# First two operands of the third product's batch 0 made one quarter earlier in the second product

## Chip, cores and metric

The kernel runs on one core of one Trainium2 chip. The metric is device time in microseconds (us): the median of several executions. Times in the profile are those of one profiled execution.

## What is computed

Attention with a hash mask over 2 batches, 8 heads, 768 tokens and 64 dims, then two feed-forward layers on the 1536 x 512 result. This case lies in the feed-forward part:

```python
def _moe_ref(x, w1, w2, w3, w_out):
    h = np.maximum(np.maximum(x @ w1, x @ w2), x @ w3)
    return (h @ w_out).astype(np.float32)

def _moe2_ref(x, w_in, w_out):
    h = x @ w_in
    relu6 = np.clip(h + 3.0, 0.0, 6.0)
    g = h * relu6 / 6.0
    return (g @ w_out).astype(np.float32)

x = np.ascontiguousarray(attn_out.transpose(0, 2, 1, 3)).reshape(B * S, H * D)
x = _moe_ref(x=x, **moe_kwargs)
return _moe2_ref(x=x, **moe2_kwargs)
```

## The kernel before

Every fp32 matrix is kept as two parts in a matmul type, a high part (a copy by ScalarE into that type) and a low part (the matrix less its high part, by VectorE or GpSimd). A product of two matrices is three matmuls: high by high, high by low, low by high. The first product is `x` by `w1`, `w2`, `w3`; the second is `h` by the first layer's `w_out`; the third is the second's result by `w_in`; the fourth is the gated result by the last `w_out`.

**The second product** runs in four quarters, one for each batch `b` and half `dh` of the 512 columns, in the order `(b, dh)` = (0,0), (0,1), (1,1), (1,0). A quarter has two column tiles `d` of 128. A column tile is six steps `f` of six matmuls each (L1453, tiles `c`, `m`, `x` in PSUM), and then ScalarE copies it out into the resident tensor `xF` (L1481; in the last quarter L1473 to L1478). Four generators are advanced between the steps:

- `making` (the count a step is in `MK`, 3 in the quarters in question) makes the operands of the third product;
- `tick2` (the count is in `TQ`, by quarter, column tile and step) advances the jobs that bring weights on: `words` decodes one tile of raw words (ScalarE L954 and L956, VectorE L961 and L965) that SyncE has loaded into one of two buffers `wraw` (L918); `pjob` makes a set of seven weight operands for the third product (GpSimd L1006 and L1019, ScalarE L1015, and VectorE L1019 for the one low part that `WL` gives it); `ojob` and `wjob` make high and low parts of a plain tile (ScalarE L982 and L1070, GpSimd L984 and L1073);
- `sets0`, in the last quarter alone, runs the third product's first two sets, so that its matmuls (L1210) stand between those of the last quarter.

**The third product** multiplies blocks of 256 by 256 with seven products instead of eight (`seven`). Its right-hand operands of a batch are seven tiles of 128x768: B11, T1, T2, B21, T3, B22 and T4, of which the T's are differences of blocks. `xops` makes them one after the other, in the order that it is given:

```python
if sub:
    dve.tensor_tensor(out=B[i], in0=B[sub[0]], in1=B[sub[1]], op=ALU.subtract)    # L1161
    yield
act.activation(out=hi, in_=B[i], func=AF.Copy)                                     # L1164
yield
(dve if XE[n] else pool).tensor_tensor(out=lo, in0=B[i], in1=f32(hi), op=ALU.subtract)  # L1166
```

For batch 0 this begins at the end of the second quarter: B11 and T1 are made of the columns of the first quarter, which are in `xF` since the second quarter's beginning, and the other five also need those of the second. The differences overwrite blocks of `xF` (T1 is B12 - B11 in B11's place), and T4 is made from T2's difference. In the trace and the orders below the pairs (high, low) are B11 `xh2`/`xl2`, T1 `xh3`/`xl3`, T2 `G0`/`G1`, B21 `G2`/`G3`, T3 `T3`/`T8`, B22 `T2`/`T7`, T4 `G4`/`G5`. The third product's first set of weights is in `wh3`, `wl3`, `woh1` and others, its second in `G8` to `G11`.

`seven` starts with the product A11 by B11 in a tile `m`, ScalarE copies it to a tile `c` (L1216), and the next product is added onto that copy; a product into another tile `x` lies between, which ScalarE copies out too (L1221). VectorE then adds (L1224, L1230).

All engines take their instructions in program order. Nothing sorts them: the order of the generators' steps is the order on each engine.

Of the kernel before, what the change touches and what calls it, by code (L numbers as in the profile page):

```python
# [61 lines left out]
XS = 0  # L62
WL = (1, 0, 0, 0, 0)
WH = 2
TQ = (((2, 1, 2, 1, 2, 1), (2, 1, 2, 1, 2, 1)), ((1, 1, 1, 1, 1, 2), (1, 1, 1, 1, 1, 1)), ((1, 1, 1, 1, 1, 1), (1, 1, 1, 1, 1, 1)), ((1, 1, 1, 1, 0, 1), (1, 0, 2, 1, 1, 1)))
TS = 0
IS = 2
PR = (3, 4)
# [22 lines left out]
NW = 8  # L91
PJ = 4
LAGO = 1
XO = ((0, 1, 2, 3, 4, 5, 6),)
TN = (0, 1, 1)
OG = (1, 1, 1, 1)
PSB = (("s", 2, 2), ("x", 1, 1), ("m", 3, 1))
# [2 lines left out]
def f32(ap):  # L100
    return ap if ap.dtype == F32 else ap.bitcast(F32)
# [3 lines left out]
def body(ctx, tc, qT, kT, vP, projT, wts, consts, out):  # L105
# [26 lines left out]
    def units(tags=None):  # L132
        if not tags:
            tags = ring["order"][ring["n"] % len(ring["order"])]
            ring["n"] += 1
        if len(tags) == 2:
            return [unit(t) for t in tags]
        t = unit(tags)
        return [t[:, 0, :], t[:, 1, :]]
# [12 lines left out]
    def hsl(hf):  # L152
        return slice(hf * HF, (hf + 1) * HF)
# [101 lines left out]
    def blk(b, n):  # L255
        return X[:, 4 * b + 2 * (n // 2):4 * b + 2 * (n // 2) + 2, hsl(n % 2)]
# [665 lines left out]
    def moe(es, yp, wo, wx):  # L922
# [227 lines left out]
        def xops(b, tl, order):  # L1150


            B = [blk(b, n) for n in range(4)] + [blk(1 - b, n) for n in range(2)]
            S = (
                ("B11", 0, None), ("T1", 0, (1, 0)), ("T2", 4, (3, 0)), ("B21", 2, None),
                ("T3", 1, (3, 1)), ("B22", 3, None), ("T4", 5, (2, 4)),
            )
            for n in order:
                k, i, sub = S[n]
# [3 lines that stand above are left out]
                hi, lo = (x.rearrange("p (a b) -> p a b", a=2) for x in tl[n])  # L1163
# [3 lines that stand above are left out]
                x2[b][k] = tuple([x[:, i, :] for i in range(2)] for x in (hi, lo))  # L1167
                yield
# [129 lines left out]
        def xlate(places):  # L1298

            for k, n in (("T3", 1), ("T4", 2)):  # L1300
                B = blk(1, n)
                t = [[x[:, 0:HF] for x in places.pop(0)] for _ in range(2)]
                for j in range(2):
                    act.activation(out=t[j][0], in_=B[:, j, :], func=AF.Copy)
                    yield
                yield
                for j in range(2):
                    if j:
                        yield
                    dve.tensor_tensor(out=t[j][1], in0=B[:, j, :], in1=f32(t[j][0]), op=ALU.subtract)  # L1310
                xa[1][k] = tuple([t[j][i] for j in range(2)] for i in range(2))
                yield

        xt = [list(zip(xh0, xl0)), [(T[4], T[9]), (T[0], T[5]), (G[0], G[1]), (G[2], G[3])]]
        free = G[4:]
# [36 lines left out]
        def xmake():  # L1352
            for _ in range(4):
                yield
            thi(0, "T4")
            yield
            for k in ("T1", "T3"):
                xsum(1, k)
                yield
                yield  # L1360
            tlo(0, "T4", dve)
            yield
            for k in ("T2", "T4"):
                xsum(1, k)
                yield
            for k in ("T1", "T2"):
                thi(1, k)
                yield
                yield
                tlo(1, k, dve)  # L1370
                yield

        making = xmake()
# [27 lines left out]
        while lanes:  # L1401
            for i, g in enumerate(list(lanes)):
                if step < 24 - LN and i:
                    continue
                while next(lanes[i], 0) == 0:
                    if i == 0 and not late:
                        for _ in making:
                            pass
                        making, late = itertools.chain(hsplits.pop(0), xlate([*Wsl[3:6], wo[2]])), True
# [25 lines left out]
        def wout(i, last):  # L1435
            if last and i not in done_w:
                done_w.add(i)
                slots.append(weight2(("w", i)))
            return weight2(("w", i))

        making = iter(())
        g0, g1 = [], []
        sets0 = itertools.chain(inset(0, 0, g0, "m", "x"), inset(1, 0, g1, "m", "x"))
        for b, dh in ((0, 0), (0, 1), (1, 1), (1, 0)):
            for d in (2 * dh, 2 * dh + 1):
                us = units(("cc", "mm")[d] if (b, dh) == (1, 0) else None)
                for f in range(6):
                    wh, wl = wout(18 + 3 * dh + f // 2, b == 1 and d % 2 and f % 2)
                    c = slice(256 * (f % 2) + 128 * (d % 2), 256 * (f % 2) + 128 * (d % 2) + 128)
                    a, l = hT[f, b]  # L1450
                    for i, (w, r) in enumerate(((wh, a), (wh, l), (wl, a))):
                        for u, rh in zip(us, r):
                            pe.matmul(  # L1453
                                u[:, 0:HF], w[:, c], rh, start=f + i == 0, stop=f == 5 and i == 2
                            )
                    for _ in range(MK[3 * b + dh - 2 * b * dh]):
                        next(making, None)
                    tick2(TQ[3 * b + dh - 2 * b * dh][d % 2][f])
                    if (b, dh) == (1, 0) and 6 * d + f >= IS:
                        for _ in range(IN[6 * d + f - IS]):  # L1460
                            next(sets0, None)
                if (b, dh) == (1, 0):

                    if d == 0:
                        for _ in making:
                            pass
                        hi, lo = (
                            x.rearrange("p (a b) -> p a b", a=2) for x in (free.pop(0), free.pop(0))
                        )
                        x2[1]["B11"] = tuple([x[:, j, :] for j in range(2)] for x in (hi, lo))  # L1470
                    u0, u1 = (u[:, 0:HF] for u in us)
                    b11, t1, t3, b22 = (blk(1, n)[:, d, :] for n in (0, 0, 1, 3))
                    act.activation(out=hi[:, d, :], in_=u0, func=AF.Copy)  # L1473
                    act.activation(out=b11, in_=u0, func=AF.Copy)
                    dve.tensor_tensor(out=lo[:, d, :], in0=u0, in1=f32(hi[:, d, :]), op=ALU.subtract)
                    dve.tensor_tensor(out=b11, in0=u1, in1=b11, op=ALU.subtract)
                    dve.tensor_tensor(out=t3, in0=b22, in1=u1, op=ALU.subtract)
                    dve.tensor_tensor(out=blk(0, 0)[:, d, :], in0=u0, in1=t3, op=ALU.add)  # L1478
                    continue
                for hf in range(2):  # L1480
                    act.activation(out=X[:, 4 * b + d, hsl(hf)], in_=us[hf][:, 0:HF], func=AF.Copy)  # L1481
            if (b, dh) == (0, 0):
                while ("w", 23) not in held2:
                    tick2()
                h2 = slots.pop(0)
                s4 = wo[1]
                pslots.append({
                    "A": wo[0], "B": slots.pop(0), "S2": tuple(x[:, 0:256] for x in h2),
                    "S1": tuple(x[:, 0:256] for x in s4), "S4": tuple(x[:, 256:512] for x in s4),
                })  # L1490
            if (b, dh) == (0, 1):
                for _ in making:
                    pass
                making = xops(0, [(free.pop(0), free.pop(0)) for _ in range(7)], XO[0])
                free += own[0]
                a, b_ = ((free.pop(0), free.pop(0)) for _ in range(2))
                pslots.append({
                    "A": tuple(x[:, 0:512] for x in a), "B": tuple(x[:, 0:512] for x in b_),
                    "S1": tuple(x[:, 512:768] for x in a), "S4": tuple(x[:, 512:768] for x in b_),
                    "S2": tuple(x[:, 256:512] for x in h2),  # L1500
                })
            if (b, dh) == (1, 1):
                oslots += [slots.pop(0), slots.pop(0)]
                for _ in making:
                    pass
                tl = {n: (free.pop(0), free.pop(0)) for n in (3, 5)}
                making = xops(1, tl, (3, 5))
                g0 += [(free.pop(2), free.pop(2)) for _ in range(2)]
# [6 lines left out]
        making = xrest(1, tl)  # L1515
# [157 lines left out]
```

## Time and profile before

| | us |
|---|---|
| median of 3 executions | 688.95 (688.47 to 689.98) |
| the profiled execution | 690.18 |
| its span (first to last instruction) | 688.40 |
| TensorE matmuls busy | 666.0 (97%) |
| VectorE busy | 511.0 (74%) |
| ScalarE busy | 432.8 (63%) |
| GpSimd busy | 334.3 (49%) |
| mean granted clock of TensorE | 0.993 |

The profile has a page of sums, and the trace behind it can be asked for the waits (who waited for whom, in all), the chain of waits (the work that ended last, followed back), a timeline of single instructions, and the busy time of each engine in chosen stretches with TensorE's granted clock. In a timeline a bracket behind a row gives the idle time of the engine ahead of that row and what ended it. TensorE's matmuls overlap: they take 0.33 us each and start 0.17 us apart.

### The profile page before, as it was taken

Reading aid. Unit: us, or ns where it says so; the run is one execution under the profiler, and the core shown is the slowest. Engines: PE = TensorE matmul, PEld = TensorE weight load, DVE = VectorE, ACT = ScalarE, POOL = GpSimd, SP = SyncE. Lnnn points to the kernel's source line nnn. Section 1 sums busy time; section 2 is a strip of 40 time slices with the busy share of each in tenths; the row PEclk is TensorE's granted clock in tenths of the full one; section 3 lists DMA queues with packets and bytes.
Section 4 is the critical chain, followed back from the end, with each engine's and each line's share of the span. In section 5 each row is a group of like instructions: output and inputs, shape, how many; then the busy total and the mean of one; then the engine's idle time right before and its main releaser. Section 6 shows DMA issues by size and latency. Waiting matters only on the chain.

```text
span 688.4 us, 13482 instructions
## 1 busy us (share of the span) xinstructions
PE 666.0 (97%) x5189; PEld 613.2 (89%) x5189; DVE 511.0 (74%) x978; ACT 432.8 (63%) x749; POOL 334.3 (49%) x280
## 2 busy tenths in 40 slices
PE   8999999999999999999999996999999999999997
PEld 7789898888898989999999996989989889889986
DVE  6888988989985647677668477773868687877664
ACT  6667788889887525574746556676556565655520
POOL 6778898999987330654443543112142331313100
PEclk9999999999999999999999998999999999999999
DMA  6665557767441000211223222010203020211004
GB/s 191 170 153 136 160 123 184 191 167 190 103 90 63 2 1 32 92 62 62 62 92 120 96 64 89 31 62 1 92 30 123 31 92 31 92 61 62 1 0 184
DMA packets 22527, 61.80 MB, mean 90 GB/s; under 512 B 3864, under 2 KB 4952, under 8 KB 22464
## 3 DMA queue, kind: packets, MB, share of 16 engines
q1 hardware_dynamic: 22032, 60.55, 30.7%
q8 instruction: 41, 0.67, 0.4%
q10 hardware_dynamic: 432, 0.40, 0.2%
q14 instruction: 22, 0.18, 0.1%
HBM read 38.87 MB, written 3.15 MB: 61 GB/s over the span
## 4 chain that ended last, share of the span: by engine, by line
PE 63%; DVE 6%; ACT 2%; issue 1%; POOLq 0%; DVEq 0%; ACTq 0%
PE c L1210 16%; PE m L1210 11%; PE x L1536 10%; PE m L1536 9%; PE c L147 4%; PE m L307 3%; PE m L1453 2%; PE s L664 2%; PE c L1453 2%; PE x L1210 1%; DVE xF L1161 1%; PE x L698 1%; PE x L699 1%; PE x L700 1%; DVE mx L618 1%
## 5 line engine op out<-in xcount | busy, mean ns | idle before, releaser
L686 POOL TENSOR_TENSOR pl<-E,ph 128x768 f16<-128x768 f32 x85 | 152.4, 1808 | 30.4 <-ACT ph L671 17.2
L618 DVE TENSOR_REDUCE mx<-m 128x1 f32<-128x384 f32 x192 | 96.6, 546 | 12.3 <-PE m L614 11.4
L668 ACT ACTIVATE E<-s 128x768 f32<-128x768 f32 x96 | 78.1, 813 | 39.1 <-PE s L664 31.4
L671 ACT ACTIVATE ph<-s 128x768 f16<-128x768 f32 x85 | 68.9, 810 | 0.0
L698 PEld LDWEIGHTS <-ph 128*128 128x128 f16 x576 | 53.9, 98 | 16.3 <-issue 10.2
L698 PE MATMUL x<-VV,ph 128*128 128x65 f16 x576 | 64.5, 195 | 2.8 <-DVE xo L718 1.9
L699 PE MATMUL x<-VV,ph 128*128 128x65 f16 x576 | 64.1, 196 | 0.0
L700 PE MATMUL x<-VV,pl 128*128 128x65 f16 x576 | 63.7, 193 | 0.0
L614 PE MATMUL m<-T,T 76*128 76x384 f32 x192 | 54.0, 352 | 3.5 <-DVE mx L618 1.5
L664 PE MATMUL s<-QB,KB 128*128 128x384 f32 x192 | 56.7, 376 | 0.4 <-ACT ph L671 0.4
L699 PEld LDWEIGHTS <-ph 128*128 128x128 f16 x576 | 54.5, 98 | 0.7 <-issue 0.6
L700 PEld LDWEIGHTS <-pl 128*128 128x128 f16 x576 | 54.7, 99 | 0.0
L664 PE MATMUL s<-T,T 98*128 98x384 f32 x192 | 49.7, 340 | 0.3 <-DMA T<-mr 0.2
L1006 POOL TENSOR_TENSOR hF<-hF 128x256 f32<-128x256 f32 x8 | 6.6, 819 | 76.6 <-DVE hF L965 76.6
L614 PEld LDWEIGHTS m<-T,T 76*128 76x128 f32 x192 | 35.0, 188 | 9.6 <-DVE mx L618 5.7
L961 DVE SCALAR_TENSOR_TENSOR wy<-wy,wr 128x512 int32<-128x512 int32 x32 | 23.0, 718 | 25.9 <-ACT wr L956 25.9
L1554 DVE TENSOR_TENSOR xF<-x,xF 128x512 f32<-128x512 f32 (+1 forms) x43 | 29.4, 684 | 11.6 <-PE x L1536 11.5
L984 POOL TENSOR_TENSOR wl<-wy,wh 128x512 fp32r<-128x512 f32 x10 | 13.2, 1323 | 50.8 <-ACT wh L982 50.8
L1094 POOL TENSOR_TENSOR hF<-hF 128x256 f32<-128x256 f32 x6 | 6.5, 1090 | 62.7 <-DVE hF L1048 62.7
L664 PEld LDWEIGHTS s<-T,T 98*128 98x128 f32 x192 | 34.9, 189 | 0.9 <-DMA T<-mr 0.9
L984 POOL TENSOR_TENSOR wol<-wy,woh 128x512 fp32r<-128x512 f32 x6 | 8.0, 1342 | 51.6 <-ACT woh L982 51.6
L1252 ACT ACTIVATE gr<-m,half 128x384 f32<-128x384 f32 x30 | 17.4, 579 | 24.1 <-DVE m L1230 13.5
(472 smaller groups left out, 2198.2 us busy)
## 6 DMA issues: line engine op xcount, KB each, us to landing
wraw<-in_wts_dram SPq DMA_DIRECT2D x56, 512.0 KB
xF<-in_vP_dram SPq DMA_DIRECT2D x8, 384.0 KB
KB<-kH SPq DMA_DIRECT2D x15, 192.0 KB
QB<-qL SPq DMA_DIRECT2D x15, 192.0 KB
T<-kH SPq DMA_DIRECT2D x15, 192.0 KB
T<-qH SPq DMA_DIRECT2D x15, 192.0 KB
KB<-kL SPq DMA_DIRECT2D x15, 192.0 KB
QB<-qH SPq DMA_DIRECT2D x15, 192.0 KB
```

The lines of the kernel that those rows point to most:

```text
L614: pe.matmul(u[:, 0:HF], QA[h % NA][0:76, qt * 128:qt * 128 + 128], KA[h % NA][0:76, hsl(hf)], start=True, stop=True,)
L618: dve.tensor_reduce(out=mx[h][:, qt, hf:hf + 1], in_=u[:, 0:HF], axis=AX.X, op=ALU.max)
L664: pe.matmul(u[:, k, 0:HF], a[0:n, c], b[0:n, hsl(hf)], start=n == 128, stop=n < 128)
L668: act.activation(out=e, in_=u[:, :, 0:HF], func=AF.Exp, scale=BIG)
L671: act.activation(out=ph.rearrange("p (a b) -> p a b", a=2), in_=u[:, :, 0:HF], func=AF.Exp, scale=BIG,)
L686: eng.tensor_tensor(out=pl, in0=e, in1=ph, op=ALU.subtract)
L698: pe.matmul(o, ph[:, c], vv[:, 0:65], start=kt == 0, stop=False)
L699: pe.matmul(o, ph[:, c], vv[:, 65:130], start=False, stop=False)
L700: pe.matmul(o, pl[:, c], vv[:, 0:65], start=False, stop=False)
L1210: pe.matmul(u, l[:, s], r[i], start=first and i + j == 0, stop=i == 1 and j == 2, skip_group_check=not first,)
L1536: pe.matmul(u[:, 0:c1 - c0], (h, l, h)[k], (oh, oh, ol)[k][:, c0:c1], start=j == k == 0, stop=j == 1 and k == 2,)
L1554: dve.tensor_tensor(out=o, in0=u[:, 0:c1 - c0], in1=o, op=ALU.add)
```

## The change

`xops` for batch 0 is started at the end of the first quarter, with the seven pairs of tiles taken there, and makes B11 and T1 in the second quarter; the other five follow from the end of the second quarter, as before. In the third quarter's second column tile the weight jobs get three ticks, at every other step, in place of six.

```diff
-TQ = (((2, 1, 2, 1, 2, 1), (2, 1, 2, 1, 2, 1)), ((1, 1, 1, 1, 1, 2), (1, 1, 1, 1, 1, 1)), ((1, 1, 1, 1, 1, 1), (1, 1, 1, 1, 1, 1)), ((1, 1, 1, 1, 0, 1), (1, 0, 2, 1, 1, 1)))
+TQ = (((2, 1, 2, 1, 2, 1), (2, 1, 2, 1, 2, 1)), ((1, 1, 1, 1, 1, 2), (1, 1, 1, 1, 1, 1)), ((1, 1, 1, 1, 1, 1), (1, 0, 1, 0, 1, 0)), ((1, 1, 1, 1, 0, 1), (1, 0, 2, 1, 1, 1)))
...
-XO = ((0, 1, 2, 3, 4, 5, 6),)
+XO = ((0, 1), (2, 3, 4, 5, 6))
...
             if (b, dh) == (0, 0):
+                xo = [(free.pop(0), free.pop(0)) for _ in range(7)]
+                making = xops(0, xo, XO[0])
...
             if (b, dh) == (0, 1):
                 for _ in making:
                     pass
-                making = xops(0, [(free.pop(0), free.pop(0)) for _ in range(7)], XO[0])
+                making = xops(0, xo, XO[1])
```

No instruction is added or taken away on any engine, and the order of matmuls, of GpSimd's instructions and of the loads is the same. ScalarE and VectorE change places of instructions between the second quarter's beginning and the third product's first matmuls.

The first place is the beginning of the second quarter, on ScalarE and then on VectorE:

```order
 L1481 ACTIVATE xF_96<-m_6413 128x384
+L1164 ACTIVATE xh2_99<-xF_96 128x768
 L1015 ACTIVATE wh3_113<-hF0_105 128x512
+L1164 ACTIVATE xh3_100<-xF_96 128x768
 L1015 ACTIVATE woh1_5202<-hF1_106 128x256
```

ScalarE makes the high parts of B11 and T1 directly behind the copies of the first quarter's second tile; they stood behind the copies of the second quarter's second tile.

```order
 L965 SCALAR_TENSOR_TENSOR hF1_106<-wraw_6385,wy_5277 128x512
-L1019 TENSOR_TENSOR wl3_114<-hF0_105,wh3_113 128x512
-L961 SCALAR_TENSOR_TENSOR wy_5277<-wy_5277,wr_6516 128x512
-L965 SCALAR_TENSOR_TENSOR hF0_105<-wraw_6422,wy_5277 128x512
-L961 SCALAR_TENSOR_TENSOR wy_5277<-wy_5277,wr_6551 128x512
-L965 SCALAR_TENSOR_TENSOR hF1_106<-wraw_6447,wy_5277 128x512
 L1166 TENSOR_TENSOR xl2_103<-xF_96,xh2_99 128x768
 L1161 TENSOR_TENSOR xF_96<-xF_96 128x2x384
 L1166 TENSOR_TENSOR xl3_104<-xF_96,xh3_100 128x768
+L1019 TENSOR_TENSOR wl3_114<-hF0_105,wh3_113 128x512
```

On VectorE the two low parts and T1's difference now stand ahead of five instructions of the weight jobs that they stood behind; after these comes T2's difference.

The second place is around T4, the last operand, in the third quarter, on VectorE:

```order
 L1166 TENSOR_TENSOR T7_93<-xF_96,T2_88 128x768
+L1161 TENSOR_TENSOR xF_96<-xF_96 128x2x384
+L965 SCALAR_TENSOR_TENSOR wy_5278<-wraw_6541,wy_5277 128x512
+L1166 TENSOR_TENSOR G5_5217<-xF_96,G4_5216 128x768
 L1019 TENSOR_TENSOR G9_5221<-hF0_105,G8_5220 128x512
-L1161 TENSOR_TENSOR xF_96<-xF_96 128x2x384
-L1166 TENSOR_TENSOR G5_5217<-xF_96,G4_5216 128x768
 L961 SCALAR_TENSOR_TENSOR wy_5277<-wy_5277,wr_6650 128x512
```

The weight set's low part `G9` stood ahead of T4's difference (L1161) and now stands behind T4's low part.

The third place is the same stretch on ScalarE:

```order
 L1015 ACTIVATE G10_5222<-hF1_106 128x512
-L1164 ACTIVATE T3_89<-xF_96 128x768
+L1164 ACTIVATE G4_5216<-xF_96 128x768
 L1015 ACTIVATE G10_5222<-y2_5234 128x256
-L1164 ACTIVATE T2_88<-xF_96 128x768
 L982 ACTIVATE woh2_5204<-wy_5278 128x512
-L1164 ACTIVATE G4_5216<-xF_96 128x768
```

T4's high part `G4` stood behind two weight copies (a 128x256 to `G10`, a 128x512 to `woh2`) and now stands ahead of them; from there to L1216 the order is as it was.

## Rows read from the trace of the kernel before

**Rows 1.** TensorE's waits in the whole span: us in total, times, longest
```profile
PE c L1210 <- ACT c L1216: 5.3, 1, 5.3
...
PE c L1210 <- DVE c L1224: 1.2, 2, 0.8
```

**Rows 2.** Chain of waits, second quarter's end to the stall: start, us, what
```profile
398.92 0.74 ACT xh L1164
...
399.68 1.04 DVE xl L1166
...
400.75 1.38 DVE xF L1161
...
403.04 0.96 DVE xl L1166
403.99 1.43 DVE xF L1161
...
414.17 1.70 DVE G L1019
...
417.32 0.85 ACT G L1164
...
419.28 1.52 ACT xF L1481 x4
...
421.53 0.52 ACT wh L982
...
422.78 0.55 ACT wy L954
...
423.88 0.39 ACT c L1216
```

**Rows 3.** The same chain on TensorE, from the stall on
```profile
424.31 2.29 PE c L1210 x6
426.60 1.92 PE m L1453 x6
428.52 1.55 PE m L1210 x6
430.08 1.04 PE m L1453 x6
```

**Rows 4.** Timeline of TensorE, the last matmul ahead of the stall
```profile
418.65 0.34 PE L1453 MATMUL c<-T,wol 128*128 128x384 f32 x1
```

**Rows 5.** Stretches: length, PE, PEld, DVE, ACT, POOL busy, PEclk, DMA share, GB/s
```profile
412.00:415.00 3.00, 3.00 (x19) 3.00 (x18) 2.75 (x3) 1.70 (x4) 1.22 (x1) 1.00 0.55 175
415.00:421.00 6.00, 3.99 (x23) 3.67 (x22) 4.63 (x5) 3.68 (x8) 1.47 (x2) 1.00 0.00 0
422.00:423.00 1.00, 0.00 (x0) 0.00 (x0) 0.71 (x2) 1.00 (x3) 0.88 (x1) 0.84 0.76 295
424.30:429.90 5.60, 5.58 (x18) 5.59 (x19) 4.07 (x8) 2.90 (x6) 1.29 (x1) 0.53 0.28 94
440.00:444.00 4.00, 3.19 (x18) 2.88 (x17) 3.20 (x6) 2.53 (x5) 0.00 (x0) 1.00 0.01 4
```

**Rows 6.** Timeline of ScalarE, VectorE and GpSimd, second and third quarters
```profile
385.57 0.88 ACT L1481 ACTIVATE xF<-m 128x384 f32<-128x384 f32 x2
...
392.08 1.59 DVE L961 SCALAR_TENSOR_TENSOR wy<-wy,wr 128x512 int32<-128x512 int32 x1 [4.39 <-ACT wr L956]
...
396.88 0.69 DVE L965 SCALAR_TENSOR_TENSOR hF<-wraw,wy 128x512 int32<-128x512 int32 x1
...
408.45 2.00 POOL L1019 TENSOR_TENSOR G<-hF,G 128x512 fp32r<-128x512 f32 x1
409.23 2.03 DVE L1161 TENSOR_TENSOR xF<-xF 128x768 f32<-128x768 f32 x1
```

**Rows 7.** Timeline of SyncE's load, and of ScalarE's one wait for a load
```profile
384.33 0.67 ACT L954 ACTIVATE wy<-wraw 128x512 f32<-128x512 f32 x1 [1.02 <-DMA wraw<-in_wts_dram]
...
411.93 0.33 SPq L918 DMA_DIRECT2D wraw<-in_wts_dram  x1
```

## The prediction

> **What bounds the kernel now.** TensorE is busy for 97% of the span (the table above), so a change off its path is worth only what TensorE waits for. I therefore read its waits first [rows 1]: the longest of all is 5.3 us, once, for ScalarE's copy at L1216. The chain of waits, followed back from there, shows what that copy waited for [rows 2]: it leaves TensorE at the copies that end the second quarter (398.92 us) and returns at 424.31, and in between runs over VectorE and ScalarE alone. For these 25 us the seven operands of batch 0 are made one after the other, and ScalarE, which takes its instructions in order, reaches L1216 only behind T4's high part (417.32), four copies out of PSUM (419.28) and further copies. TensorE began its last matmul ahead of the stall at 418.65 [rows 4]; matmuls start 0.17 us apart, so the next could have started at 418.82. It started at 424.31: **5.49 us lost**.
>
> The stall has a second price. The stretches [rows 5] show the granted clock at 0.84 in the microsecond from 422 and at 0.53 from 424.3 to 429.9: between the levels of 2.4 and 1.2 GHz, TensorE spent these microseconds almost wholly on the lower one after it had been idle. Three groups of six matmuls took 2.29 + 1.92 + 1.55 = 5.76 us there, where the next group of six, at full clock, took 1.04 [rows 3]. At full clock they are 3 x 1.04 + 0.16 (the first matmul's overlap) = 3.28. **2.48 us lost**.
>
> **The change, part by part.** Nothing is added or removed, so each term is a place in the chain. All moments are of the profiled execution, whose 690.18 us lie 1.23 above the median; I take differences from it off the median of 688.95.
>
> *Out of the chain: B11 and T1.* High and low part of B11, T1's difference, its high and its low part are the five pieces from 398.92 to 403.99 [rows 2]. Behind the change T2's difference is the first thing to be done when the second quarter's last copies have landed, at 398.92 + 0.02. That is **-5.05**, if VectorE is free by then.
>
> *Whether it is.* The five pieces now start behind the first quarter's copies, which end at 385.57 + 0.88 = 386.45 [rows 6], and take 5.07: to about 391.5. VectorE stood idle for 4.39 us until 392.08 there, which hides most of them. Behind them VectorE still has one weight part (128x512, as the 0.69 at 396.88) that it used to do earlier, and ScalarE has four copies and a decode of raw words behind T1's high part, so that VectorE's weight work starts 1.0 to 1.3 us later. Its last instruction ended at 396.88 + 0.69 = 397.57, so there are 1.35 us of room before 398.92. I take the slip as hidden, with 0 to 1.0 for the range. TensorE needs nothing of this until 413 us. The copies out of PSUM of the second quarter's first tile slip by about 1 us too; their banks are next written in the last quarter, from 410.5.
>
> *Out of the chain: the weight part G9.* VectorE's L1019 (1.70, at 414.17 [rows 2]) stood ahead of T4's difference and now stands behind T4's low part: **-1.70**.
>
> *Into the chain.* Two weight copies stood ahead of T4's high part, where ScalarE waited anyway, and now stand behind it, ahead of L1216: a 128x512, like the one of 0.52 at 421.53, and a 128x256, which cannot be longer. Bounds 0.52 and 1.04; I take **+0.8**. The copy at 421.53 (L982) needs VectorE's decode, which now stands behind G9: 1.70 more on VectorE against 0.8 more on ScalarE, of which a part was slack. Bounds 0 and 1.70; I take **+0.4**, near the lower end, since ScalarE's four copies at 419.28 (1.52) stand ahead of it as well.
>
> *VectorE beside GpSimd.* VectorE's difference at 409.23 took 2.03, its like at 400.75 1.38 [rows 2, 6]; the long one began while GpSimd's instruction from 408.45 to 410.45 ran, and ended 0.81 after it. The moved work meets GpSimd's instructions at other points. Between the shortest such piece of VectorE (0.96) and 2.03 the bound for one meeting is 1.07 either way; I take **+0.3** for all of them together, since most meetings only change their partner. The Trainium skill's page "SBUF — State Buffer", section "Who interferes with whom", says that a VectorE instruction with two SBUF inputs and a GpSimd instruction share a read interface, and that whichever starts first keeps the other out until it ends. The trace agrees in these two rows. By that rule alone each of VectorE's three moved instructions would be held up in the second quarter, where GpSimd makes weights, the slip would pass its room by up to 0.8, and the sum would give 682.0; by the idle row it is 681.2, which I keep.
>
> *Ticks.* Three ticks fewer in the third quarter help to set where the weight jobs' instructions stand; the places counted above contain that. GpSimd's order and SyncE's do not change.
>
> *The sum.* L1216 started at 423.88: 423.88 - 5.05 - 1.70 + 0.8 + 0.4 + 0.3 = **418.63**. TensorE started 0.43 behind it (424.31), so now at 419.06, with a wait of 0.24 in place of 5.49: -5.25. So short a wait leaves the clock: in the stretch from 440 to 444 TensorE stood still for 0.8 us and kept 1.00 [rows 5]. So the 2.48 go too. Together **-7.73**: span 680.7, and for the median 688.95 - 7.73 = **681.2**.
>
> *What is late next.* The bounds of the wait are 0 (TensorE then runs through, 7.97 gained, 681.0) and, with every term at its bad end, 423.88 - 5.05 + 1.0 - 1.70 + 1.04 + 1.70 + 1.07 + 0.43 = 422.37, a wait of 3.55 and 684.5 if the clock stays. In the slow stretch VectorE had 4.07 us of work [rows 5]; at full clock there are 3.28, so 0.8 moves on. VectorE has 0.8 idle from 440 to 444, and TensorE's next wait there, for L1224 [rows 1], follows on TensorE's own matmuls. I cost it at nothing; without that cover it is 0.8, inside the range.
>
> **Rivals.** *The chain is still late.* If the slip passes its room, or GpSimd is met at bad points, a wait of 1 to 3.5 us stays. For it: the way to T4 has many terms of about a microsecond, and the sum ends only 0.2 beside TensorE. At 2.5 the gain is 2.99 + 2.48 = 5.47: 683.5.
>
> *The clock does not come back.* The waits that are left would then cost TensorE its full clock all the same: the 5.25 are won, the 2.48 are not, 683.7. Against it: full clock in the stretch with the 0.8 us wait [rows 5]. The Trainium skill's "TensorE: Matmul & The Clock Gate", section "A second HAM failure mode: psum-queue depth-cycling", says that frequent short pauses between groups of matmuls made the clock swing between its levels in another kernel; the trace does not bear that out for one pause of this length.
>
> *The move is paid back in the second quarter.* If VectorE's weight work slipped so far that T2's difference started at 403.99 as before, the wait would only move into the weight jobs. It would take 1.35 + 5.05 = 6.4 us of slip from five pieces of 5.07 that meet 4.39 of idle time. The time would stay within about 1 us, at 688.5.
>
> *Slower: ScalarE blocked by a load.* The decode copy L954 (422.78) stands two places ahead of L1216, and needs raw words that SyncE loads only when VectorE has freed the buffer. Before, that load left at 411.93, transfers ran until 415 and none until 421 [rows 5, 7], so it took about 3.1, hidden by 7.8 us. Now it leaves at about 411, and ScalarE is at L954 by 417.5. If the load took longer than 422.78 - 411 = 11.8 us, TensorE would start later than before; at 14 us it is 2.2 later, 691.1. For it: ScalarE did wait once for such a load, 1.02 us at 384.33. Against it: 3.1 is far from 11.8.
>
> **How the numbers follow.** Forecast (a wait of 0 to 1) 0.78; chain still late 0.11; clock 0.04; paid back 0.04; load 0.03. Predicted time 681.2. The range goes from 680.4 (no wait, 681.0, less 0.6, as single runs of before lie 0.5 under to 1.0 over their median) to 683.7 (a wait of about 2.7, or the clock's case), which leaves out a tenth. A measurement can tell 0.2% (1.4 us) from no change. The first three cases are faster by more than that: 0.93. Paid back is within it, 0.04, the load slower, 0.03.
>
> **What would show it.** TensorE's wait for L1216 is gone from its list or under 1 us; no stretch of granted clock under 1.00 between 410 and 440; T2's difference starts at about 399 and T4's high part near 410.5; L1216 starts near 418.6; VectorE's 4.39 us idle in the second quarter is mostly filled. A wait of over 1 us for L1216, or one on a load or on VectorE of like size in that place, would make the forecast wrong.

## The result and the profile after

| | before | after |
|---|---|---|
| median of 4 executions each, us | 688.71 (688.18 to 689.98) | 681.35 (680.07 to 681.51) |
| ratio | | 0.9886 (95%: 0.9868 to 0.9905) |
| the profiled execution, us | 690.18 | 680.07 |
| its span, us | 688.40 | 678.30 |
| TensorE matmuls busy, us | 666.0 (97%) | 662.5 (98%) |
| VectorE, ScalarE, GpSimd busy, us | 511.0, 432.8, 334.3 | 510.2, 432.5, 338.2 |
| mean granted clock | 0.993 | 0.997 |

The change makes the kernel 7.4 us faster; 681.2 was forecast. In a later run the changed kernel was measured again (see the experiments); its profiled execution took 1644.78 us, and no figure here uses it. The profiled execution of after lies 1.28 us below its median, that of before 1.47 above (the median of four), so the two traces differ by more than the medians do, by 10.11 us. They can be split at one point, the last matmul of the second quarter, which started at 397.84 before and at 395.49 after. The 2.35 us ahead of it come from a part of the program in which the change moves nothing. From there to the end it was 290.56 us (688.40 - 397.84) and is 282.81: **7.75 us**, where the prediction's sum has 7.73. The difference of the medians is 7.36. Moments of after are set beside those of before by adding 2.35.

The longest wait of the kernel is gone. In the list of TensorE's waits in after there is no row for L1216; of the two of [rows 1] this is left:

```profile
PE c L1210 <- DVE c L1224: 1.2, 2, 0.8
```

The chain of waits of after, from the last copies of the second quarter to the third product's first matmuls (start, us, engine, tile and line):

```profile
395.70 0.88 ACT xF L1481 x2
...
396.60 0.97 DVE xF L1161
...
406.51 1.98 DVE xF L1161
...
408.52 0.85 ACT G L1164
409.37 0.30 ACT G L1015
409.67 0.52 ACT woh L982
...
411.35 1.33 DVE wy L961
...
412.76 1.07 DVE wy L965
...
413.85 0.63 ACT wh L982
...
416.35 0.38 ACT c L1216
...
416.77 1.33 PE c L1210 x6
418.11 1.04 PE m L1453 x6
419.14 1.04 PE m L1210 x6
```

Against [rows 2], B11 and T1 are no longer in it: T2's difference follows 0.02 behind the copies. T4's high part (408.52) goes to ScalarE ahead of the two weight copies (409.37, 409.67). L1216 starts at 416.35 and TensorE at 416.77, 0.42 behind it. TensorE's last matmul ahead of that started at 416.30, so the next could have started at 416.47: it waited **0.30 us**, in place of 5.49. The list of waits and the brackets of a timeline count otherwise, from the end of the last matmul (416.30 + 0.34): by them the wait is 0.13 us after and 5.33 before, and the waits of the experiments below are read in this way. The groups of six take 1.33, 1.04 and 1.04 where [rows 3] have 2.29, 1.92 and 1.55.

The same stretch of time in the table of engines (length; PE, PEld, DVE, ACT and POOL busy; then PEclk, DMA share, GB/s):

```profile
415.00:419.00 4.00, 3.86 (x23) 3.54 (x22) 3.29 (x4) 3.04 (x7) 1.05 (x2) 1.00 0.35 121
419.00:421.00 2.00, 2.00 (x13) 2.00 (x13) 1.48 (x3) 2.00 (x5) 1.10 (x1) 1.00 0.77 258
421.00:425.00 4.00, 4.00 (x25) 4.00 (x24) 3.44 (x8) 2.08 (x5) 0.00 (x0) 1.00 0.01 2
```

The granted clock is 1.00 where [rows 5] have 0.84 and 0.53. VectorE's timeline in the second quarter shows where the moved pieces went:

```profile
384.85 1.43 DVE L1166 TENSOR_TENSOR xl<-xF,xh 128x768 fp32r<-128x768 f32 x1 [0.21 <-ACT xh L1164]
386.31 1.38 DVE L1161 TENSOR_TENSOR xF<-xF 128x768 f32<-128x768 f32 x1
388.61 1.20 DVE L1166 TENSOR_TENSOR xl<-xF,xh 128x768 fp32r<-128x768 f32 x1 [0.91 <-ACT xh L1164]
389.73 1.23 DVE L1019 TENSOR_TENSOR wl<-hF,wh 128x512 fp32r<-128x512 f32 x1
391.18 0.93 DVE L961 SCALAR_TENSOR_TENSOR wy<-wy,wr 128x512 int32<-128x512 int32 x1 [0.22 <-ACT wr L956]
...
395.08 0.69 DVE L961 SCALAR_TENSOR_TENSOR wy<-wy,wr 128x512 int32<-128x512 int32 x1 [1.28 <-ACT wr L956]
395.87 0.69 DVE L965 SCALAR_TENSOR_TENSOR hF<-wraw,wy 128x512 int32<-128x512 int32 x1
...
396.60 0.96 DVE L1161 TENSOR_TENSOR xF<-xF 128x768 f32<-128x768 f32 x1
```

And two rows of GpSimd's timeline there:

```profile
385.54 2.75 POOL L1006 TENSOR_TENSOR hF<-hF,hF 128x256 f32<-128x256 f32 x2
...
396.64 1.52 POOL L1006 TENSOR_TENSOR hF<-hF 128x256 f32<-128x256 f32 x1 [2.24 <-DVE hF L965]
```

The 4.39 us idle of [rows 6] are filled. VectorE's last weight instruction ends at 396.56 (395.87 + 0.69), 398.91 in the time of before, where it ended at 397.57: a slip of 1.34 us into a room of 1.35. T2's difference starts 0.04 behind it. The copies landed at the same moment (396.57), so nothing was lost, but 0.01 us of the room is all that is left.

### The profile page after: what moved, and what is told of

Same layout as the page of the kernel before. It is cut to its first block, busy times and chain, and to the rows that moved or that the text cites. A ratio compares the mean times of both kernels' runs of the same rounds, so it can differ in the third digit from the quotient of the medians.

```text
span 678.3 us, 13481 instructions
## 1 busy us (share of the span) xinstructions
PE 662.5 (98%) x5189; PEld 611.0 (90%) x5189; DVE 510.2 (75%) x978; ACT 432.5 (64%) x749; POOL 338.2 (50%) x280
## 4 chain that ended last, share of the span: by engine, by line
PE 63%; DVE 6%; ACT 2%; issue 1%; POOLq 0%; DVEq 0%; ACTq 0%
PE c L1210 16%; PE m L1210 11%; PE x L1538 10%; PE m L1538 9%; PE c L147 4%; PE m L307 3%; PE m L1453 2%; PE s L664 2%; PE c L1453 2%; PE x L1210 1%; PE x L698 1%; DVE xF L1161 1%; PE x L699 1%; PE x L700 1%; DVE mx L618 1%
## 5 line engine op out<-in xcount | busy, mean ns | idle before, releaser
L1006 POOL TENSOR_TENSOR hF<-hF 128x256 f32<-128x256 f32 x8 | 6.9, 859 | 75.5 <-DVE hF L965 75.5
L961 DVE SCALAR_TENSOR_TENSOR wy<-wy,wr 128x512 int32<-128x512 int32 x32 | 23.0, 718 | 22.0 <-ACT wr L956 22.0
L984 POOL TENSOR_TENSOR wl<-wy,wh 128x512 fp32r<-128x512 f32 x10 | 13.0, 1298 | 46.4 <-ACT wh L982 46.4
L984 POOL TENSOR_TENSOR wol<-wy,woh 128x512 fp32r<-128x512 f32 x6 | 8.4, 1393 | 50.9 <-ACT woh L982 50.9
L1556 DVE TENSOR_TENSOR xF<-m,xF 128x512 f32<-128x512 f32 (+1 forms) x42 | 28.5, 678 | 4.6 <-PE m L1538 4.6
```

Source lines behind the costliest of these rows:

```text
L1556: dve.tensor_tensor(out=o, in0=u[:, 0:c1 - c0], in1=o, op=ALU.add)
```

## The experiments

The theory is the prediction's. The stall was the length of one chain from the second quarter's copies to L1216, and it cost its own length and then TensorE's clock; the change takes pieces out of the chain and hides them in VectorE's idle time. The rivals: that only one part of the change matters, that the clock would have come back by itself, and that the gain has another bound (VectorE's work, or the next wait). Each kernel below is one edit, or one on top of another; those with added instructions write a tile that is not used afterwards.

**B11 alone moved.** Against after:

```diff
-XO = ((0, 1), (2, 3, 4, 5, 6))
+XO = ((0,), (1, 2, 3, 4, 5, 6))
```

> The changed kernel, but only B11 is made in the second quarter; T1's difference, high and low part (403.99 - 400.75 = 3.24 us of the chain before) stay in the chain behind it. Theory (the gain is the wait for L1216, plus the clock's price if the wait is long): L1216 starts 3.2 us later than in the changed kernel, TensorE waits about 3.5 us there; 684.6 us if the clock stays at 1.00 through such a wait, 687.1 if it falls as it did before the change (there it fell about 3.7 us after the last matmul, so this run lies at the edge). Rival (the gain came from G9's new place or from the earlier start alone, not from the length of the chain): within 1 us of the changed kernel's 681.35.

Measured: 683.0 us (682.32 to 684.06), ratio to before 0.9923 (0.9908 to 0.9938). Its wait for L1216, in TensorE's timeline:

```profile
418.80 0.62 PE L1210 MATMUL c<-G,wh 128*128 128x384 f32 x2 [1.73 <-ACT c L1216]
```

The stretches around it, with the columns as above:

```profile
416.00:420.00 4.00, 2.27 (x14) 1.95 (x13) 3.51 (x4) 3.16 (x6) 1.42 (x1) 1.00 0.39 131
420.00:424.00 4.00, 4.00 (x25) 4.00 (x24) 3.08 (x7) 2.98 (x6) 1.30 (x1) 1.00 0.41 131
```

The wait is half of what was expected, because T1's difference needs only columns of the first quarter. VectorE began it before the second quarter's copies had ended, and was done 0.13 us behind them (two rows of the timeline of VectorE and ScalarE):

```profile
396.18 0.95 DVE L1161 TENSOR_TENSOR xF<-xF 128x768 f32<-128x768 f32 x1
...
396.51 0.49 ACT L1481 ACTIVATE xF<-x 128x384 f32<-128x384 f32 x1
```

Only T1's high and low part stay in the chain. From the end of the copies to L1216 it takes 21.38 us (397.00 to 418.38), in after 19.78 (396.57 to 416.35). The 1.60 more are the wait's 1.60 more (1.73 against 0.13), and the median is 1.65 above that of after. So the length of the chain sets the wait, and moving T1 matters; the rival (within 1 us of after) is ruled out, and the size that I gave T1's move was wrong. And the clock stays at 1.00 behind a wait of 1.73.

**Five and fifteen copies ahead of L1216.** Against after, ScalarE makes extra copies of 128x256 between the first product and L1216, in the third product's first set:

```diff
+            if not alone and not q2.get("late"):
+                q2["late"] = 1
+                for _ in range(5):                # 15 in the other kernel
+                    act.activation(out=prH, in_=f32(prL), func=AF.Copy)
             act.activation(out=c, in_=a, func=AF.Copy)
```

> The changed kernel with five extra copies of 128x256 on ScalarE directly ahead of L1216 (their result is not used). Each costs 0.30 to 0.41 us by the weight copies of that size: 1.5 to 2.05 in all. Theory (a short wait leaves the clock): TensorE's wait for L1216 is 1.8 to 2.4 us, granted clock 1.00 behind it, time 682.9 to 683.4. Rival (any wait left there costs TensorE its full clock): the same wait, the clock near 0.5 for some 5 us behind it, 685.3 to 685.9.

> The same with fifteen such copies, 4.5 to 6.2 us. Theory (a wait of the length of the one before brings back the clock's price of about 2.5 us as well): wait 4.8 to 6.5, clock near 0.5 for some 5 us behind it, time 688.3 to 690.1. Rival (the clock's price is no part of the gain): 685.9 to 687.5 with the clock at 1.00.

Measured with five: 684.7 us (683.47 to 685.34), ratio 0.9944 (0.9928 to 0.996). The wait, in TensorE's timeline:

```profile
420.71 1.01 PE L1210 MATMUL c<-G,wh 128*128 128x384 f32 x2 [2.66 <-ACT c L1220]
```

The microseconds from then on:

```profile
420.00:421.00 1.00, 0.29 (x1) 0.29 (x2) 0.00 (x0) 1.00 (x4) 0.00 (x0) 0.59 0.09 33
421.00:422.00 1.00, 1.00 (x4) 1.00 (x4) 0.00 (x0) 1.00 (x4) 0.35 (x1) 0.50 0.88 180
422.00:423.00 1.00, 1.00 (x5) 1.00 (x4) 0.00 (x0) 1.00 (x3) 0.94 (x1) 0.50 0.76 311
423.00:424.00 1.00, 1.00 (x5) 1.00 (x5) 0.90 (x2) 0.46 (x1) 0.00 (x0) 0.71 0.00 0
```

This wait of 2.66 us took the clock: 0.50 is the level of 1.2 GHz. So the expectation that such a wait leaves the clock was wrong here, and the rival's mechanism was seen, at a smaller price than it named. The wait is above its 1.8 to 2.4 us because the five copies took 2.10 us together (418.18 to 420.28 in the chain), not 1.5 to 2.05, and T2's difference 1.51 beside GpSimd, in after 0.97. The first two groups of six took 2.29 + 1.37 us against 1.33 + 1.04 in after, 1.29 more; with the wait's 2.53 that is 3.82, and the medians differ by 3.35. One of the four executions has a mean granted clock of 1.000, and it is the fastest (683.47): its record shows no fall, so the clock did not fall in every execution.

Measured with fifteen: 690.48 us (688.8 to 691.92, 10 executions), ratio 1.0025 (1.0011 to 1.004). The wait, in the list of TensorE's waits:

```profile
PE c L1210 <- ACT c L1220: 7.1, 1, 7.1
```

The stretches behind it show the clock low for longer:

```profile
424.00:427.00 3.00, 0.39 (x1) 0.40 (x2) 0.00 (x0) 2.88 (x8) 0.00 (x0) 0.50 0.02 8
427.00:430.00 3.00, 3.00 (x11) 3.00 (x11) 1.00 (x3) 2.36 (x5) 1.29 (x1) 0.50 0.00 0
430.00:431.00 1.00, 1.00 (x5) 1.00 (x4) 0.97 (x4) 0.00 (x0) 0.00 (x0) 0.62 0.00 0
```

Wait and time lie above what was expected (4.8 to 6.5 and 688.3 to 690.1), the time by 0.4 us; the fifteen copies took 6.58 us, and T2's difference took 1.53 here too. The run is 9.1 us over after, and 7.0 of that are the longer wait (7.14 against 0.13). Against before, whose wait was 5.33, it waits 1.8 longer and is 1.9 slower (690.48 - 688.54): with the wait put back nothing is left of the gain, so within this noise the stall and the clock behind it are the whole of it.

**G9 alone, on the kernel before.** The one weight part that stood on VectorE ahead of T4 goes to GpSimd; nothing else changes:

```diff
-                (dve if WL[n] else pool).tensor_tensor(
+                (dve if WL[n] and x != ("p", 1) else pool).tensor_tensor(
```

> The kernel before, with one instruction moved: the weight part G9 (128x512, 1.70 us of the chain) is made by GpSimd, not by VectorE; the five pieces of B11 and T1 stay where they were. Theory: 1.70 out of the chain, TensorE's wait for L1216 3.8 us in place of 5.5 and 687.0 us if the clock still falls, up to 2.5 less if it does not; GpSimd's extra 1.3 us can meet VectorE's work and give back up to 1.1. Rival (G9 is no part of what sets L1216, the five pieces are all): 688.7.

Measured: 687.18 us (686.07 to 687.97, 10 executions), ratio 0.9975 (0.9965 to 0.9985). The wait for L1216 falls from 5.3 to 4.3, not by the 1.70 that G9's piece was long. The timeline shows who took the rest: T4's difference now meets GpSimd's L984 and takes 2.05 (1.49 in the timeline of before).

```profile
411.83 1.54 POOL L984 TENSOR_TENSOR wol<-wy,woh 128x512 fp32r<-128x512 f32 x1 [3.34 <-ACT woh L982]
...
412.14 2.05 DVE L1161 TENSOR_TENSOR xF<-xF 128x768 f32<-128x768 f32 x1
```

The median is 1.36 us under that of before (688.54). Part of this is the clock: behind the wait of 4.29 us the first three groups of six took 4.95 us (2.10 + 1.81 + 1.04), where before had 5.76. So G9's place is a real but small part of the gain. In after, G9 took 0.69, so of its 1.70 in [rows 2] about a microsecond was meeting GpSimd, whose L984 ran from 413.78 to 415.32 there.

**After again, and with T4 earlier.** The changed kernel itself was run again, beside a version that makes T2, T3, T4 first and B21, B22 behind them:

```diff
-XO = ((0, 1), (2, 3, 4, 5, 6))
+XO = ((0, 1), (2, 4, 6, 3, 5))
```

> The changed kernel itself again, as the yardstick for the two behind it on the same chip: 681.4 us, TensorE's wait for L1216 0.2 to 0.4 us, clock 1.00 from 400 us on.

> The changed kernel with the five later operands in the order T2, T3, T4, B21, B22, so that the last difference does not stand at the end of the chain. Theory (ScalarE's way to L1216 is what TensorE waits for, and 0.3 us is all that is left): the wait for L1216 goes to 0, 681.1 us, no difference that 5 rounds tell. Rival (TensorE's start there is set by VectorE's amount of work, not by the order of the operands): the wait stays at 0.3. A gain of over 1 us would mean that the wait shown is not all that this stretch still loses.

Measured for the changed kernel: 680.83, 681.43, 683.54, 684.38 and 684.63 us, ratio 0.9901 (0.9877 to 0.9926). Two of the five are at the 681.4 that was expected, three are 2 to 3 us above it; the two slowest have the lowest mean granted clocks (0.994 and 0.992), but no trace shows where. By the median of these five the gain is 6.1 us (689.59 - 683.54); the interval of its ratio overlaps that of the first measurement. The wait and the clock expected here were not read.

For the reordered one: 681.76 (681.11 to 683.05), ratio 0.9884 (0.9865 to 0.9904). The intervals overlap, so the two can't be told apart. In the reordered kernel's trace the wait did not go to 0; the chain shows what took T4's place:

```profile
414.77 0.71 DVE wy L965
...
415.50 0.63 ACT wh L982
...
417.98 0.39 ACT c L1216
...
418.42 1.32 PE c L1210 x6
```

ScalarE waits for VectorE's decode L965, which comes behind G9, and G9 takes 1.80 beside GpSimd (timeline of both):

```profile
411.69 1.30 POOL L984 TENSOR_TENSOR wol<-wy,woh 128x512 fp32r<-128x512 f32 x1 [2.16 <-ACT woh L982]
411.74 1.80 DVE L1019 TENSOR_TENSOR G<-hF,G 128x512 fp32r<-128x512 f32 x1
```

TensorE waits 0.90. With T4 early, VectorE's work and its meetings with GpSimd set L1216, so the rival comes nearer than the theory, though the wait grew where it had it stay. This one other order gives nothing that could be told.

**The next wait.** On top of that order, the last quarter's last step takes four steps of `sets0` in place of two, which takes away the two waits for L1224:

```diff
-IN = (1, 0, 1, 1, 1, 1, 1, 1, 0, 2)
+IN = (1, 0, 1, 1, 1, 1, 1, 1, 0, 4)
```

> The same, and the third product's second set is taken two steps further ahead of the last quarter's copies out of PSUM, so that VectorE's L1224 stands ahead of L1475 to L1478. That is the next wait of TensorE, 0.8 us once and 0.4 a little later. Theory (these waits are what is late next, and they are all that is left there): 0.8 to 1.2 us less than the run before it, 680.0 to 680.5. Rival (VectorE is the bound of that stretch, 8.4 of 10 us busy, and the wait only changes its place): the same time, with a wait of like size at a later matmul.

Measured: 687.15 us (683.79 to 688.63, 10 executions), ratio 0.996 (0.9942 to 0.9977). The waits for L1224 are gone, and three others stand there (timeline of TensorE):

```profile
435.88 1.33 PE L1210 MATMUL c<-G,G 128*128 128x384 f32 x6 [0.48 <-DVE x L1230]
...
440.79 0.44 PE L1210 MATMUL c<-wh,wh 128*128 128x384 f32 x1 [1.49 <-ACT wh L1179]
...
442.68 0.55 PE L1210 MATMUL c<-wh,wh 128*128 128x384 f32 x1 [1.44 <-DVE wh L1182]
```

The stretches behind the last two:

```profile
442.00:443.00 1.00, 0.32 (x1) 0.33 (x2) 1.00 (x3) 0.67 (x1) 0.00 (x0) 0.93 0.00 0
443.00:444.00 1.00, 1.00 (x5) 1.00 (x5) 0.09 (x1) 0.00 (x0) 0.00 (x0) 0.50 0.00 0
```

TensorE's matmuls moved forward, but VectorE and ScalarE, which make the operands for L1210, did not get faster: TensorE runs into them, twice within 2 us, and loses the clock. The wait changed its place, as the rival had it, but the time did not stay the same: it is 5.4 us longer than the reordered kernel's. The profiled execution is only 3.0 us over the reordered kernel's and the median 5.4; what the other executions lost more was not seen in a trace.

**The second quarter filled up.** Against after, VectorE gets four extra differences of 128x256 behind T1's low part:

```diff
+                if (b, n) == (0, 1):
+                    for _ in range(4):
+                        dve.tensor_tensor(out=prL, in0=f32(prH), in1=f32(prH), op=ALU.subtract)
```

> The changed kernel with four extra differences of 128x256 on VectorE in the second quarter, behind T1's low part (their result is not used), 0.35 to 0.45 us each, 1.4 to 1.8 in all. Theory (the change used up the room of 1.35 us in that quarter: T2's difference began 0.04 us behind VectorE's last weight instruction): T2's difference and L1216 come 1.4 to 1.8 later, TensorE's wait is 1.7 to 2.1, time 682.8 to 683.2, and up to 1.8 more where such a wait also takes the clock. Rival (the second quarter still has room, since VectorE waits there for ScalarE): 681.4, wait 0.3.

Measured: 684.06 us (681.98 to 685.36), ratio 0.9916 (0.9887 to 0.9944). VectorE's timeline:

```profile
391.32 4.16 DVE L1170 TENSOR_TENSOR prL<-prH 128x256 fp32r<-128x256 f32 x4
...
400.15 0.95 DVE L1161 TENSOR_TENSOR xF<-xF 128x768 f32<-128x768 f32 x1
```

TensorE's wait, in the list:

```profile
PE c L1215 <- ACT c L1221: 2.1, 1, 2.1
```

The four took 4.16 us, not the 1.4 to 1.8 expected; GpSimd's L1019 ran beside them from 390.55 to 395.20 almost without a break. Of these, idle time behind them took up about half, and the wait grew by 2.0 us (2.10 against 0.13). From T2's difference to the copy in L1216's place it takes 19.62 us (400.24 to 419.86), in after 19.75: the chain keeps its length and only starts later. So the room in the second quarter is used up. This is read from the trace: the time alone can't be told from the changed kernel's in the same run (683.54, the intervals overlap). The clock stayed at 1.00 behind this wait.

## Why the prediction was right

Each step was looked for in the trace of after (+2.35 us where it is a moment).

- *Out of the chain, B11 and T1* (-5.05): T2's difference starts at 396.60, that is 398.95, where 398.94 was forecast.
- *The slip is hidden*: 1.34 measured, "1.0 to 1.3 us" forecast, in a room of 1.35. It held by 0.01, so the forecast was right here by luck in the last step: a slip 0.02 larger would have begun to use the 0 to 1.0 that was kept for the range.
- *From T2's difference to T4's high part* (-1.70 for G9, +0.3 for GpSimd, together -1.40): 403.99 to 417.32 was 13.33, 396.60 to 408.52 is 11.92, so -1.41. That it comes out to 0.01 is luck, since two misses cancel. The weight copy of 0.30 (128x256, to `G10`) that left this stretch stood in the chain of before at 412.14, and not where ScalarE waited anyway; and the rest, where +0.3 was taken for meetings with GpSimd, came to about +0.6 (T2's difference 0.46 shorter, T3's 0.55 shorter, T4's 0.56 longer, the high and low parts together 1.05 longer).
- *From T4's high part to L1216* (+0.8 + 0.4): 6.56 before, 7.83 after, +1.27. The two copies took 0.30 + 0.52 = 0.82 in the chain. The decode copy L982 did wait for VectorE's L965, with 0.3 us of idle time, but not because L965 stands behind G9: G9 ended at 410.96, and VectorE then waited for ScalarE until 411.35. The decode itself was longer: L961 and L965 took 1.33 and 1.07 us, against 0.69 each before, beside GpSimd's instructions from 410.27 to 413.26. The +0.4 has the right size for another reason.
- *L1216 and TensorE*: 418.70 and 419.12 against 418.63 and 419.06; the wait is 0.30 against 0.24, so 5.19 of its 5.49 us are gone, where 5.25 was forecast.
- *The clock* (-2.48): 1.00 throughout. The first three groups took 3.41 us (1.33 + 1.04 + 1.04) against 5.76, which is 2.35. Wait and clock together are 7.54; the other 0.21 of the 7.75 lie behind this stretch.
- *The load*: no wait of ScalarE for a load stands in this stretch.

Four things in the working were weaker than the total lets them look.

*The bound of the range.* "A wait of 3.55 and 684.5 if the clock stays", and "at 2.5 the gain is 2.99 + 2.48", took the clock as safe up to 3.55 us, on the evidence of one pause of 0.8. It fell behind 2.66. If it falls behind the rival's 2.5 too, which no run shows, then with the low clock's price in the run with five copies (1.3 us) the rival's 683.5 becomes 684.8 (with five copies it was 684.7) and lies outside the range. For a forecast at 0.24 it made no difference; half a microsecond here and there more, and it would have.

*Short waits.* The page "TensorE: Matmul & The Clock Gate" of the Trainium skill, section "A second HAM failure mode: psum-queue depth-cycling", was set aside with the words "the trace does not bear that out for one pause of this length". For one pause that stands (0.90, 1.73 and 2.10 us kept 1.00). For two it does not: behind 1.49 and 1.44 us with one matmul between them the clock fell. Here the trace goes with that page, though the page speaks of frequent pauses and a clock that swings, and this is two pauses and one fall.

*VectorE beside GpSimd.* The Trainium skill's rule in "SBUF — State Buffer", section "Who interferes with whom", was costed at 682.0 and passed over for the idle row. The moved instructions were indeed held up: B11's low part took 1.43 and T1's 1.20, where the chain of before has 1.04 and 0.96. VectorE's idle time took most of this up: the slip was 1.34, and T2's difference lost nothing. So rule and row both held, the rule for each instruction and the row for the sum. Not counted at all was the other side: GpSimd's pair from 385.54 took 2.75, and its busy time in the whole span grew by 3.9 us; no engine waited for GpSimd in this stretch.

*Ticks.* "Three ticks fewer in the third quarter help to set where the weight jobs' instructions stand": they don't. Built with the change to `TQ` alone, the program has the order of before on every engine, and with `XO` and `xops` alone that of after (neither was run). This part of the change does nothing.

What stays open is behind which waits the clock falls. It kept 1.00 behind 0.13, 0.90, 1.73 and 2.10 us and fell behind 2.66, 4.29, 5.33 and 7.14, each read from one profiled execution; at 2.66 one other execution shows no fall.

## What to carry to other kernels

When one long wait ends a chain over several engines, write the chain down with the moment from which each piece *could* start: here two of seven operands had had their inputs for a whole quarter, and the gain is their time in the chain, the pieces that change places with them, and the clock that the stall took. Then check the room where they go, to a tenth of a microsecond, with the other engine's hold-ups in it. Once the wait is near 0, stop at this chain: the next edits at the same place, another order and an earlier start of the matmuls, ran into the work of VectorE and ScalarE and gained nothing that could be told or lost 5 us against the version that it was made from.

## What was not expected of the hardware

- **How long the clock stays low comes in two sizes here.** It was low for about 3.4 us with the waits of 2.66 (420.2 to 423.6) and 4.29 (421.4 to 424.9), and for about 6.8 us with those of 5.33 in before (422.7 to 429.5) and 7.14 (423.9 to 430.8). A longer wait thus cost more than its length: about 1.3 us of slower matmuls behind the first, 2.5 in before. Each is one profiled execution.
- **Which of VectorE and GpSimd is held up depends on which began first.** At 396.60 VectorE began and took 0.96, and GpSimd's L1006, 0.04 behind it, took 1.52 where the same instruction takes 0.73 to 0.74 undisturbed. At 405.66 GpSimd began (timeline of after), and T4's difference ended 0.83 behind the end of GpSimd's instruction:

```profile
405.66 2.00 POOL L1019 TENSOR_TENSOR G<-hF,G 128x512 fp32r<-128x512 f32 x1
...
406.44 2.05 DVE L1161 TENSOR_TENSOR xF<-xF 128x768 f32<-128x768 f32 x1
```

- **A stretch at half clock stands early in nearly every trace,** not at one place: in before around 48 us, in after around 28 us, about 3.4 us long in both; in the trace of the next wait there is none ahead of 440. The change moves nothing there, so two traces are better compared from a point behind it, as was done above.
